# A fused attention and expert kernel: queries, keys and values laid out head dimension first

## The chip, the cores and the metric

The kernel runs on one core of one Trainium2 chip. The metric is the device time of one execution in microseconds (us). The kernel before takes 1295.8 us as the median of 3 runs (1295.32 to 1297.02).

## What is computed

Four batches of 12 heads, 448 tokens, head dimension 64. The scores of all heads are mixed across heads before the softmax (`w_pre`), and the weights again after it (`w_post`). The result feeds a layer of 8 experts, one per token, and then a dense layer of 2048. All arithmetic is in float32.

```python
def _attn_ref(q, k, v, w_pre, w_post):
    scale = 1.0 / np.sqrt(q.shape[-1])
    scores = scale * np.matmul(q, k.transpose(0, 1, 3, 2))
    scores = np.einsum('bhij,hg->bgij', scores, w_pre)
    scores = scores - np.max(scores, axis=-1, keepdims=True)
    attn = np.exp(scores)
    attn = attn / (np.sum(attn, axis=-1, keepdims=True) + 1e-09)
    attn = np.einsum('bhij,hg->bgij', attn, w_post)
    return np.matmul(attn, v).astype(np.float32)

def reference(...):
    attn_out = _attn_ref(**attn_kwargs)
    x = attn_out.transpose(0, 2, 1, 3).reshape(B * S, H * D)
    x = _moe_ref(x=x, **moe_kwargs)      # argmax expert, gate * (relu(x @ w1[e]) @ w2[e])
    return _moe2_ref(x=x, **moe2_kwargs) # (h - tanh(h)) @ w_out, h = x @ w_in
```

## The kernel before, in words

The kernel has four stretches: a prologue (loads, keys of batch 0, the first scores), an attention loop, the experts, and the dense layer. The change touches the prologue and the attention loop alone.

Attention is cut into 16 query tiles T (four per batch, of 120, 120, 120 and 88 queries). For each tile, S (`emit_S`, line 316) makes the scores of two heads at a time as a product of head dimension 64: both heads of pair p lie one above the other on the 128 partitions. To keep float32 accuracy each operand is cut into a rounded part `hi` and a rest `lo`, and three products are added (line 330). The parts come from `tr_k` (line 283, once per batch and pair: 24 calls) and `tr_q` (line 297, two halves per tile: 32 calls). Queries and keys arrive token first, so both turn them on TensorE with an identity (lines 287 and 303; 4 turns in a call of `tr_k`, 3 in one of `tr_q`) into a PSUM bank; ScalarE then copies the bank to `hi` (lines 293, 310) and VectorE subtracts to get `lo` (lines 294, 311).

The scores of 10 queries by 12 heads form a block of 120 rows, which a DMA on SP's queue (`emit_relay`, line 358, kept NSR = 8 blocks ahead) brings into shape. There are NBK = 180 blocks, and the loop (line 1149) runs one step per block. In step s TensorE's program order is: P(s) (line 373: heads mixed with `w_pre`), then one filling (S, or AV: the weighted sum of values, line 430), then T(s-2) (line 412: heads mixed with `w_post` and the block turned, LAG = 2 steps behind), then the turns of that step (`turns`, line 1176), then X (line 464) where one is due. VectorE in a step: the maximum of P(s) (line 377), `emit_W` for block s-1 (lines 387 to 390), a piece of the dense weights' rounding (`conv_do`, lines 117 to 119) in some steps, and the `lo` parts, deferred through `late2`. ScalarE: exp(s) (line 380), the `hi` parts, the copies of T (line 417) and AV (line 432).

Which step does what is written out by hand before the loop: `at(pos, fn, ...)` puts a call into a step, `at_e` into the next step that has no other user of the bank "e". `posS2(T, p)` and `posAV(T, p)` give the steps of S and AV. Lines 1007 to 1015 place the loads of q (6 steps ahead of the tile's first S), the turns of q, the loads of k (5 steps ahead of its turns) and the turns of k. `conv_do` is spread over 72 steps (lines 1035 to 1048), preferring those with AV or S.

The prologue (lines 1114 to 1148) does a little idle work on TensorE (`warm`, line 216, a product of the identity with itself), turns k and q of tile 0, and makes the scores of tile 0 and a third of tile 1. When the last pair of tile 0 is there, `relay_to` starts the first relays.

In the prologue and in the loop alike, q comes in a DMA whose pieces are 64 floats (line 147), and k in two DMAs per pair, one per head (line 152).

## Time and profile before

| | |
|---|---|
| median of 3 runs | 1295.8 us |
| profiled execution, its own time | 1295.99 us |
| its span in the profile | 1294.1 us |
| TensorE busy | 1283.5 us (99%) |
| VectorE busy | 1003.8 us (78%) |
| ScalarE busy | 747.7 us (58%) |
| GpSimd busy | 489.4 us (38%) |
| attention loop | about 19.5 to 500 us of the span |

PE is TensorE's products, PEld its weight loads, which run beside the products; DVE is VectorE, ACT ScalarE, POOL GpSimd, SP the engine that issues most DMAs. The end of a product is modelled in the profile, and products overlap: what a group of products holds up of the next is read from start to start, not from the durations.

### The profile page before, as it was taken

Reading aid. Unit: us, or ns where it says so; the run is one execution under the profiler, and the core shown is the slowest. Engines: PE = TensorE matmul, PEld = TensorE weight load, DVE = VectorE, ACT = ScalarE, POOL = GpSimd, SP = SyncE. Lnnn points to the kernel's source line nnn. Section 1 sums busy time; section 2 is a strip of 40 time slices with the busy share of each in tenths; the row PEclk is TensorE's granted clock in tenths of the full one; section 3 lists DMA queues with packets and bytes.
Section 4 is the critical chain, followed back from the end, with each engine's and each line's share of the span. In section 5 each row is a group of like instructions: output and inputs, shape, how many; then the busy total and the mean of one; then the engine's idle time right before and its main releaser. Section 6 shows DMA issues by size and latency. Waiting matters only on the chain.

```text
span 1294.1 us, 24851 instructions
## 1 busy us (share of the span) xinstructions
PE 1283.5 (99%) x9072; PEld 1125.4 (87%) x9072; DVE 1003.8 (78%) x2168; ACT 747.7 (58%) x1513; POOL 489.4 (38%) x497
## 2 busy tenths in 40 slices
PE   9999999999999999999999999999999999999998
PEld 6777777777777778999999999999999999999997
DVE  5877877787878677788787676788888887888886
ACT  6767666666766665555544545765444556444432
POOL 1334423351344126333223222454644544444431
PEclk9999999999999999999999999999999999999999
DMA  7887665666557458778988876321211123111102
GB/s 172 268 267 214 199 204 152 200 202 192 160 168 223 147 157 301 262 264 250 268 245 259 265 241 210 105 86 49 86 58 65 49 99 122 50 50 49 50 25 88
DMA packets 153077, 210.95 MB, mean 163 GB/s; under 512 B 57686, under 2 KB 113158, under 8 KB 152950
## 3 DMA queue, kind: packets, MB, share of 16 engines
q1 hardware_dynamic: 149680, 195.37, 49.1%
q0 software_dynamic: 2480, 12.19, 2.7%
q8 instruction: 74, 1.21, 0.4%
q10 hardware_dynamic: 790, 1.74, 0.4%
q14 instruction: 53, 0.43, 0.1%
HBM read 135.71 MB, written 35.01 MB: 132 GB/s over the span
## 4 chain that ended last, share of the span: by engine, by line
PE 94%; DVE 2%; DMA 2%; ACT 1%; issue 0%; POOL 0%; SPq 0%; DVEq 0%; POOLq 0%
PE T L412 12%; PE P L373 10%; PE AV L430 6%; PE o L1454 6%; PE o L1452 6%; PE o L1453 6%; PE h L1418 6%; PE h L1417 6%; PE h L1416 6%; PE S L330 5%; PE ypi L706 3%; PE ypi L707 3%; PE ypi L705 3%; PE hi L729 3%; PE hi L730 3%; PE hi L731 3%
## 5 line engine op out<-in xcount | busy, mean ns | idle before, releaser
L412 PEld LDWEIGHTS T<-w,p 120*112 120x112 f32 (+1 forms) x1440 | 166.1, 177 | 59.5 <-issue 46.0
L122 POOL TENSOR_TENSOR cm<-cm,ct 128x256 f32<-128x256 f32 x96 | 70.7, 736 | 313.5 <-DVE ct L119 291.6
L412 PE MATMUL T<-w,p 120*112 120x120 f32 (+1 forms) x1440 | 185.0, 272 | 0.2 <-ACT p L380 0.2
L1399 POOL TENSOR_TENSOR gl<-th,gh 128x512 fp32r<-128x512 f32 (+1 forms) x64 | 77.5, 1211 | 241.1 <-ACT gh L1398 180.4
L373 PE MATMUL P<-sr,wpre 120*120 120x448 f32 x360 | 166.3, 544 | 1.0 <-DMA sr<-ssb 1.0
L380 ACT ACTIVATE p<-P,mx 120x448 f32<-120x448 f32 x180 | 114.1, 634 | 89.9 <-DVE mx L387 76.2
L1420 ACT ACTIVATE u<-h 128x512 f32<-128x512 f32 (+1 forms) x64 | 35.0, 547 | 204.1 <-PE h L1418 204.1
L1452 PE MATMUL o<-woh,gh 128*128 128x384 f32 x448 | 151.4, 338 | 0.0
L1454 PE MATMUL o<-woh,gl 128*128 128x384 f32 x448 | 150.4, 336 | 0.0
L1453 PE MATMUL o<-wol,gh 128*128 128x384 f32 x448 | 150.1, 335 | 0.0
L1458 DVE TENSOR_TENSOR acc<-acc,o 128x384 f32<-128x384 f32 x196 | 106.5, 548 | 47.2 <-PE o L1454 47.2
L377 DVE TENSOR_REDUCE mx<-P 120x1 f32<-120x448 f32 x180 | 111.6, 620 | 28.9 <-PE P L373 26.7
L120 POOL TENSOR_TENSOR cm<-craw 128x256 f32<-128x256 f32 x96 | 66.9, 697 | 112.8 <-DMA craw<-in_moe_w_in 59.2
L417 ACT COPY A<-T 112x480 f32<-112x480 f32 x180 | 102.3, 568 | 9.7 <-PE T L412 9.7
L729 PE MATMUL hi<-xhi,w1h 128*128 128x256 f32 x336 | 95.3, 283 | 0.0
L730 PE MATMUL hi<-xli,w1h 128*128 128x256 f32 x336 | 95.2, 283 | 0.0
L731 PE MATMUL hi<-xhi,w1l 128*128 128x256 f32 x336 | 95.2, 283 | 0.0
L705 PE MATMUL ypi<-w2hi,hhi 128*128 128x384 f32 x272 | 93.9, 345 | 0.0
L430 PEld LDWEIGHTS AV<-A,v 112*64 112x64 f32 x1536 | 73.9, 137 | 21.8 <-issue 10.7
L706 PE MATMUL ypi<-w2li,hhi 128*128 128x384 f32 x272 | 91.2, 335 | 0.2 <-DVE w2li L673 0.2
L707 PE MATMUL ypi<-w2hi,hli 128*128 128x384 f32 x272 | 91.2, 335 | 0.0
L121 POOL TENSOR_SCALAR cm<-cm 128x256 f32<-128x256 f32 x96 | 85.9, 895 | 8.4
(299 smaller groups left out, 3436.3 us busy)
## 6 DMA issues: line engine op xcount, KB each, us to landing
sr<-ssb SPq DMA_DIRECT2D x176, 210.0 KB
r<-in_moe_w SPq DMA_DIRECT2D x72, 384.0 KB
r<-in_moe_w SPq DMA_DIRECT2D x52, 512.0 KB
craw<-in_moe_w_in SPq DMA_DIRECT2D x48, 256.0 KB
craw<-in_moe_w_out SPq DMA_DIRECT2D x48, 256.0 KB
wor<-wo_d SPq DMA_DIRECT2D x16, 768.0 KB
raw<-wi_d SPq DMA_DIRECT2D x15, 768.0 KB
wi_d<-cm SPq DMA_DIRECT2D x48, 128.0 KB
```

The costliest lines, as they stand in the source:

```text
L373: pe.matmul(pt[:n, :S], wpre[:n, :n], t[:n, :], start=True, stop=True)
L412: pe.matmul(pt[:CP, c * n:(c + 1) * n] if m == 10 else pv[:, c], p[:n, c * CP:(c + 1) * CP], w[:n, :] if m == 10 else wv, start=True, stop ...
L430: pe.matmul(pt[64 * hh:64 * hh + 64, x * 120:x * 120 + n], vt[b, p + x][:, hh, c, :], A[T][:, c, 2 * (p + x) + hh, :n], start=c == 0, stop ...
L705: pe.matmul(pt[:, :384], a, wh[:, n0:n0 + 384], start=f == 0, stop=False)
L706: pe.matmul(pt[:, :384], a, wl[:, n0:n0 + 384], start=False, stop=False)
L707: pe.matmul(pt[:, :384], l, wh[:, n0:n0 + 384], start=False, stop=f == KF - 1)
L729: pe.matmul(pt[:, :256], wh[:, sl], xh[:, c, :], start=c == 0, stop=False)
L730: pe.matmul(pt[:, :256], wh[:, sl], xl[:, c, :], start=False, stop=False)
L731: pe.matmul(pt[:, :256], wl[:, sl], xh[:, c, :], start=False, stop=c == KD - 1)
L1452: pe.matmul(pt[:, :384], gh[:, sl], wo[0][:, f, n0:n0 + 384], start=f == 0, stop=False)
L1453: pe.matmul(pt[:, :384], gh[:, sl], wo[1][:, f, n0:n0 + 384], start=False, stop=False)
L1454: pe.matmul(pt[:, :384], gl[:, sl], wo[0][:, f, n0:n0 + 384], start=False, stop=f == GF - 1)
```

## The change

The host lays q, k and v out in the order in which they lie in SBUF: q and k head dimension first, with the two heads of a pair one above the other. Each load is one DMA with long pieces. `tr_q` and `tr_k` keep their names but turn nothing: `hi` is a ScalarE copy of the loaded tile (in the prologue a VectorE copy for q of tile 0), `lo` a VectorE subtraction from it. They no longer use PSUM or TensorE. From tile 3 on they are placed in steps that hold an AV (`at_av`, at most two to a step where there is a choice); there the `hi` copies follow exp(s) directly and the `lo` subtractions follow `conv_do`. q has two buffers instead of one and is loaded 9 steps ahead of its parts, k 8 steps ahead. In the prologue there are more idle products, the scores of each pair are brought to SBUF half by ScalarE and half by VectorE (`both`), and the loads of `w_pre` and `w_post` are issued earlier.

```diff
         def load_k(b, p):
-            t = ap.tile([CP, NJ, 2, D], F32, tag="natk", name=f"natk{b}_{p}", bufs=NP)
-            for hh in range(2):
-                sp.dma_start(t[:, :, hh, :], k[b, 2 * p + hh].rearrange("(p c) d -> p c d", c=NJ))
+            t = ap.tile([128, S], F32, tag="natk", name=f"natk{b}_{p}", bufs=NP)
+            sp.dma_start(t, k[b, p])
...
-        def tr_k(b, p, tag="e"):
-            src = nat.pop(("k", b, p))
-            pt = ps(tag, f"ptk{b}_{p}")
-            for c in range(NJ):
-                pe.transpose(pt[:, c * CP:(c + 1) * CP], src[:, c].rearrange("p h d -> p (h d)"), ident[:CP, :CP])
+        def tr_k(b, p, cpy=act.copy):
+            raw = nat.pop(("k", b, p))
             hi = ap.tile([128, S], F32R, tag="kh", name=f"kh{b}_{p}", bufs=6)
             lo = ap.tile([128, S], F32R, tag="kl", name=f"kl{b}_{p}", bufs=6)
             kT[b, p] = (hi, lo)
-
-            def evac():
-                act.copy(hi, pt[:, :S])
-                return lambda: dve.tensor_sub(lo, pt[:, :S], hi.bitcast(F32))
-            return evac
-
-        def tr_q(T, hf, tag="e"):
+            cpy(hi, raw)
+            return lambda: dve.tensor_sub(lo, raw, hi.bitcast(F32))
+
+        def tr_q(T, hf, cpy=act.copy):
             n = IT[T % 4][1]
-            src = nat["q", T]
-            pt = ps(tag, f"ptq{T}_{hf}")
-            for p in range(3):
-                pp = 3 * hf + p
-                pe.transpose(pt[:, p * 120:p * 120 + n], src[:n, 2 * pp:2 * pp + 2, :].rearrange("p h d -> p (h d)"), ident[:n, :n])
-            pv = pt[:, :360].rearrange("p (c i) -> p c i", c=3)[:, :, :n]
+            raw = nat["q", T][:, 3 * n * hf:3 * n * hf + 3 * n].rearrange("p (c i) -> p c i", c=3)
...
+        avs = {int(posAV(T, p)): 0 for T in range(4 * B - 1) for p in range(0, NP, 2)}
+
+        def at_av(lo, hi, fn, *a):
+            ok = [x for x in sorted(avs) if int(lo) < x < int(hi)]
+            x = ([x for x in ok if avs[x] < 2] + [min(ok, key=lambda x: avs[x])])[0]
+            avs[x] += 1
+            at(x, fn, *a)
+            return x
+
+        for T in range(3, 4 * B):
+            b, it = divmod(T, 4)
+            if it == 0:
+                for p in range(0, 4):
+                    at(at_av(posS2(T - 1, p), posS2(T, p), tr_k, b, p) - 8, load_k, b, p)
+            x = at_av(posS2(T - 1, 2), posS2(T, 0), tr_q, T, 0)
+            at_av(posS2(T - 1, 4), posS2(T, 2), tr_q, T, 1)
+            at(x - 9, load_q, T)
...
-        warm("b", 8)
+        warm("b", 16)
         pen = prep_en()
         next(pen)
-        fns = [tr_k(0, 0, "e"), tr_q(0, 0, "d")]
...
+        tr_q(0, 0, dve.tensor_copy)()
+        tr_k(0, 0)()
+        tr_k(0, 1)()
         for p in range(NP):
+            if p + 2 < NP:
+                tr_k(0, p + 2)()
             if p == 1:
...
-            if p + 2 < NP:
-                tr_k(0, p + 2, "de"[p % 2])()()
-            run_fill(emit_S, (0, p, (None, "cc", "bb")[p % 3]))
+                tr_q(0, 1, dve.tensor_copy)()
+            run_fill(emit_S, (0, p, (None, "cc", "bb")[p % 3], True))
+            warm("e", 3)
             for _ in range(2):
                 if p >= 1:
                     next(pen, None)
+            if p == 3:
+                tr_q(1, 0)()
...
             ex()
+            subs = [fn(*a) for fn, a in todo if fn in (tr_q, tr_k)]
             for fn, a in todo:
                 if fn is conv_do:
                     fn(*a)
+            for fn in subs:
+                fn()
...
-            turns = [x for x in fill if x[0] in (tr_q, tr_k)] if on else []
-            for fn, a in turns:
-                flush("e")
-                late2.append(("e", fn(*a)()))
...
+    def lay(name, a):
+        if name == "q":
+            t = a.reshape(b, h // 2, 2, s, d).transpose(0, 2, 4, 1, 3).reshape(b, 2 * d, h // 2, s)
+            return np.concatenate([t[:, :, :, x].reshape(b, 2 * d, -1) for x in parts], axis=2)
+        if name == "k":
+            return a.reshape(b, h // 2, 2, s, d).transpose(0, 1, 2, 4, 3).reshape(b, h // 2, 2 * d, s)
...
```

## Rows read from the trace of the kernel before

**Rows 1.** The page, part 1: busy time, share of the span, instructions.

```profile
PE 1283.5 (99%) x9072; PEld 1125.4 (87%) x9072; DVE 1003.8 (78%) x2168; ACT 747.7 (58%) x1513; POOL 489.4 (38%) x497
```

**Rows 2.** The page, part 4: the chain that ended last, by engine.

```profile
PE 94%; DVE 2%; DMA 2%; ACT 1%; issue 0%; POOL 0%; SPq 0%; DVEq 0%; POOLq 0%
```

**Rows 3.** Windows, the loop: PE, PEld, DVE, ACT, POOL busy (count), clock, DMA.

```profile
22.00:490.00 468.00, 468.00 (x4071) 349.53 (x4070) 358.10 (x1106) 320.17 (x761) 159.16 (x219) 1.00 0.66 199
```

**Rows 4.** Timeline, weight loads of two steps: start, length, line, tiles, count.

```profile
132.72 0.35 PEld L303 LDWEIGHTS ptq<-ident,natq 120*128 120x128 f32 x3
133.02 0.29 PEld L373 LDWEIGHTS P<-sr,wpre 120*120 120x120 f32 x2
133.97 1.63 PEld L430 LDWEIGHTS AV<-A,v 112*64 112x64 f32 x32 [0.66 <-PE ptq L303]
135.76 0.89 PEld L412 LDWEIGHTS T<-w,p 120*112 120x112 f32 x8 [0.16 <-issue]
136.57 0.29 PEld L373 LDWEIGHTS P<-sr,wpre 120*120 120x120 f32 x2
```

**Rows 5.** Timeline, weight loads: turns of 88 queries, and of a key pair.

```profile
197.27 0.32 PEld L303 LDWEIGHTS ptq<-ident,natq 88*128 88x128 f32 x3
197.53 0.29 PEld L373 LDWEIGHTS P<-sr,wpre 120*120 120x120 f32 x2
...
199.10 0.44 PEld L287 LDWEIGHTS ptk<-ident,natk 112*128 112x128 f32 x4
199.49 0.29 PEld L373 LDWEIGHTS P<-sr,wpre 120*120 120x120 f32 x2
```

**Rows 6.** Groups by line, 22 to 490 us: count, busy us, mean ns, idle.

```profile
L303 PE MATMUL ptq<-ident,natq 120*128 120x120 f32 (+1 forms) x84 | 12.6, 259 | 0.0
L287 PE MATMUL ptk<-ident,natk 112*128 112x112 f32 x72 | 9.9, 259 | 0.0
```

**Rows 7.** Timeline, VectorE: maximum, weights of a block, a rounding piece.

```profile
132.16 0.62 DVE L377 TENSOR_REDUCE mx<-P 96x1 f32<-96x448 f32 x1 [0.37 <-PE P L373]
...
133.07 0.28 DVE L390 TENSOR_SCALAR w<-wpost,mx 120x120 f32<-120x120 f32 x1
...
135.53 0.28 DVE L117 TENSOR_SCALAR ct<-craw 128x256 int32<-128x256 int32 x1
...
136.30 0.42 DVE L119 SCALAR_TENSOR_TENSOR ct<-craw,ct 128x256 int32<-128x256 int32 x1
```

**Rows 8.** Lines 293, 294, 310, 311: ns min/median/max, first and last start.

```profile
L293 ACT CAST kh<-ptk x24: 522/526/533, 6.4 to 351.6; 128x448 fp32r<-128x448 f32 x24
L294 DVE TENSOR_TENSOR kl<-ptk,kh x24: 602/625/627, 7.0 to 352.1; 128x448 fp32r<-128x448 f32 x24
L310 ACT CAST qh<-ptq x32: 379/450/465, 6.9 to 444.8; 128x360 fp32r<-128x360 f32 x24, 128x264 fp32r<-128x264 f32 x8
L311 DVE TENSOR_TENSOR ql<-ptq,qh x32: 431/532/533, 7.5 to 445.3; 128x360 fp32r<-128x360 f32 x24, 128x264 fp32r<-128x264 f32 x8
```

**Rows 9.** Lines 669, 673, the same work from SBUF, in the experts.

```profile
L669 DVE CAST w1h<-r x4: 681/686/1225, 487.3 to 496.2; 128x1024 fp32r<-128x1024 f32 x4
...
L673 DVE TENSOR_TENSOR w1l<-r,w1h x50: 1209/1219/1661, 501.3 to 788.6; 128x1024 fp32r<-128x1024 f32 x50
```

**Rows 10.** Timeline, the prologue: idle products, first turns, Exp, scores, relays, P(0).

```profile
1.43 3.49 PEld L220 LDWEIGHTS warm<-ident 128*128 128x128 f32 x16 [1.43 <-POOL dmask L174]
...
5.63 0.55 PEld L287 LDWEIGHTS ptk<-ident,natk 112*128 112x128 f32 x4 [0.72 <-DMA natk<-in_k]
5.69 0.20 ACT L261 ACTIVATE mxk<-carry 128x1 f32<-128x1 f32 x1
...
15.94 0.62 DVE L335 TENSOR_SCALAR ssb<-S 120x448 f32<-120x448 f32 x1
...
16.63 6.54 SPq L360 DMA_DIRECT2D sr<-ssb  x8
...
19.54 1.74 PE L373 MATMUL P<-sr,wpre 120*120 120x448 f32 x4 [1.02 <-DMA sr<-ssb]
```

More of the change, by code (lines that the diff above doesn't have):

```diff
@@ L30, in body @@
 @with_exitstack
-def body(ctx: ExitStack, tc, q, k, v, w_pre, w_post, emb, tau, w1, w2, win, wout, out):
+def body(ctx: ExitStack, tc, q, k, v, w_pre, w_post, emb, tau, w1, w2, win, wout, out, dims):
     nc = tc.nc
     pe, act, dve, pool, sp = nc.tensor, nc.scalar, nc.vector, nc.gpsimd, nc.sync
-    B, H, S, D = q.shape
+    B, H, S, D = dims
     NT = B * S
@@ L163, in body @@
         load_k(0, 0)
+        load_k(0, 1)
         load_q(0, 1)
-        for p in range(1, NP):
+        for p in range(2, NP):
             load_k(0, p)
+        load_q(1)
+        wr = cp.tile([120, 2, H], F32, name="wr")
+        sp.dma_start(wr[:, 0, :], w_pre.rearrange("(o h) g -> o h g", o=1).to_broadcast([10, H, H]))
+        sp.dma_start(wr[:, 1, :], w_post.rearrange("(o h) g -> o h g", o=1).to_broadcast([10, H, H]))
         act.dma_start(xbuf[1][:E], emb)
@@ L169, in body @@
         make_identity(nc, ident)
-        wr = cp.tile([120, 2, H], F32, name="wr")
         dmask = a2.tile([120, 120], F32, tag="w", name="dmask", bufs=3)[:, :10]
@@ L307, in tr_q, with emit_S @@
             qT[T, hf] = (hi, lo)
-            def evac():
-                act.copy(hi[:, :, :n], pv)
-                return lambda: dve.tensor_sub(lo[:, :, :n], pv, hi[:, :, :n].bitcast(F32))
-            return evac
+            cpy(hi[:, :, :n], raw)
+            return lambda: dve.tensor_sub(lo[:, :, :n], raw, hi[:, :, :n].bitcast(F32))
         s_sb = {}
-        def emit_S(T, p, two=None):
+        def emit_S(T, p, two=None, both=False):
             b, it = divmod(T, 4)
@@ L332, in evac @@
             def evac():
-                if two:
+                if two or both:
                     act.activation(s_sb[T][:n, 2 * p, :], pts[0][:n, :S], AF.Copy, scale=SCALE)
@@ L1007, in body @@
         for T in range(2, 4 * B):
-            at(posS2(T, 0) - 6, load_q, T)
-            at_e(posS2(T, 0) - 2, tr_q, T, 0)
-            at_e(posS2(T, 2) - 2, tr_q, T, 1)
-        for b in range(1, B):
-            for p in range(NP):
-                e = posS2(4 * b - 1, p) + 1
-                at(e - 5, load_k, b, p)
-                at_e(e, tr_k, b, p)
+            if T == 2:
+                at(1, load_q, T)
+                at(int(posS2(T, 0)) - 2, tr_q, T, 0)
+                at(int(posS2(T, 2)) - 2, tr_q, T, 1)
+        avs = {int(posAV(T, p)): 0 for T in range(4 * B - 1) for p in range(0, NP, 2)}
[13 more added lines that the diff above has]
+            at(x - 9, load_q, T)
+            if it == 0:
+                for p in range(4, NP):
+                    at(at_av(posS2(T - 1, p), posS2(T, p), tr_k, b, p) - 8, load_k, b, p)
         for p in range(NP):
@@ L1040, in body @@
         mid = [k for k in free if emit_S2 in kinds(k) and emit_AV2 not in kinds(k)]
-        alone = [k for k in long_ if not {emit_X, tr_q, tr_k} & set(kinds(k))]
+        alone = [k for k in long_ if emit_X not in kinds(k) and (tr_q not in kinds(k) and tr_k not in kinds(k))]
         more = CA - len(long_) - len(mid)
@@ L1139, in body @@
         at_e(4, tr_en)
-        PEF = (tr_q, tr_k, emit_S, emit_S2, emit_AV2, emit_X, tr_en)
-        for fn in [f() for f in (tr_q(1, 0, "e"), tr_q(1, 1, "d"))]:
-            fn()
+        PEF = (emit_S, emit_S2, emit_AV2, emit_X, tr_en)
+        tr_q(1, 1)()
         for p in range(2):
@@ L1182, in body @@
             for x in fill:
-                if x not in turns:
-                    run_fill(*x)
+                run_fill(*x)
             for fn, a in todo:
@@ L1614 @@
     from concourse.bass_utils import run_bass_kernel_spmd
+    b, h, s, d = inputs["q"].shape
+    parts = [slice(i, min(i + 120, s)) for i in range(0, s, 120)]
+    def lay(name, a):
[4 more added lines that the diff above has]
+            return a.reshape(b, h // 2, 2, s, d).transpose(0, 1, 2, 4, 3).reshape(b, h // 2, 2 * d, s)
+        if name == "v":
+            return a.reshape(b, h // 2, 2, s // 112, 112, d).transpose(0, 1, 4, 2, 3, 5).reshape(b, h // 2, 112, -1)
+        return a
     nc = bacc.Bacc("TRN2", target_bir_lowering=False, num_devices=1)
```

23 lines of the change are left out of this document (6 added, 17 removed).

## Prediction, written before the result was known

> **What bounds the kernel now.** First the busy times: TensorE is busy 99% of the span, no other engine over 78% [rows 1]. Busy products can be late products, so the chain that ended last comes second: 94% of it is TensorE, and DVE, DMA and ACT together hold 5% [rows 2]. Third the loop alone, 22 to 490 us, since the change lies there: in 468 us TensorE never stood still, VectorE worked 358.1 us (77%) and ScalarE 320.2 us (68%), at a granted clock of 1.00, the upper level of 2.4 GHz [rows 3]. What remains is whether the products stand back to back or wait for each other's operands. The timeline shows the first: in a step the weight loads of turns, P, AV, T and the next P follow at 132.72, 133.02, 133.97, 135.76 and 136.57 [rows 4]. The operands of T are there long before: the block's weights in rows 7 are ready at 133.07 + 0.28 = 133.35, and the T that reads them loads at 135.76, a margin of 2.4 us [rows 4, 7]. So in the loop TensorE's program order is the time, and an instruction taken out of it is worth the time from its start to the next one's start.
>
> **What the turns cost.** Three readings of the same rows differ, and the choice among them is the prediction. The mean duration is 259 ns for both kinds, 72 + 84 turns in the loop [rows 6], which would be 156 x 0.259 = 40.4 us. The busy time, with overlaps counted once, is 12.6 + 9.9 = 22.5 us [rows 6]. From start to start, the three turns of a 120-query half put off the next P by 133.02 - 132.72 = 0.30 us [rows 4], three of an 88-query half by 197.53 - 197.27 = 0.26 us, four of a key pair by 199.49 - 199.10 = 0.39 us [rows 5]. I take the last, because the next product doesn't wait for the end of a turn: P's weights load beside the last turns. In the loop are 84 / 3 = 28 halves of q (tiles 2 to 15: 20 of 120 queries and 8 of 88) and 72 / 4 = 18 key pairs. The sum: 20 x 0.30 + 8 x 0.26 + 18 x 0.39 = 6.0 + 2.1 + 7.0 = 15.1 us. The rest of the turns lie in the prologue, below.
>
> The Trainium skill, page "TensorE: Matmul & The Clock Gate", section "Part 4: PE-mode transpose", gives about 275 ns for a 128x128 transpose inside a kernel. Our mean of 259 ns agrees with that as a duration [rows 6]; taken as the price of one, an estimate by the page is 156 x 0.275 = 42.9 us of gain. The rows above speak against that: four turns took 0.39 us of the order [rows 5].
>
> **What takes their place in the loop.** The `hi` copies and `lo` subtractions were there before, from PSUM; now they read SBUF and stand elsewhere. From PSUM a key's `hi` takes 0.526 us, its `lo` 0.625, a query half's 0.450 and 0.532 (the 88-query halves 0.38 and 0.43, the lower ends) [rows 8]. For `lo` from SBUF the nearest row is the 1024-column subtraction with 1.219 us [rows 9], or 1.19 ns a column; the key's from PSUM is 0.625 / 448 = 1.40. By the first a key's `lo` is at least 0.53 us, by the second 0.625; I take 0.625, since the 360-column row, 1.48 ns a column, shows a fixed part that weighs more in short ones. So the work of both engines stays as it is, within 0.1 us an instruction either way.
>
> It matters where it stands. An AV step on TensorE lasts 136.57 - 133.02 = 3.55 us [rows 4]. The heaviest common load of VectorE in one is a maximum and the making of a block's weights (from 132.16 to 133.35: 1.19), a rounding piece (135.53 to 136.72: 1.19) and two key subtractions (1.25): 3.63 us [rows 7, 8]. This is level with the step, and the steps beside it hold no `lo` any more; a backlog of 1.25 us at most meets a margin of 2.4 us. ScalarE gets two copies of 0.53 us behind exp(s), ahead of the copies of AV and T, in a step of 3.55 us; at 68% it has the room. I cost both at nothing. They are hidden by the AV products. If that cover were gone, all subtractions in the loop would be on the path: 18 x 0.625 + 20 x 0.532 + 8 x 0.43 = 25.3 us.
>
> A new wait is that of ScalarE for the load itself: the `hi` copy waits for k or q, and behind it on ScalarE are the copies of AV and T, then the next exp, for which T and P wait. The loads are issued 8 or 9 steps ahead, some 21 us (the 468 us of rows 3 hold about 176 steps, 2.66 us each); the first keys had landed by 5.63 us, issued within that time [rows 10]. Nothing. On SP a pair's k is one issue instead of two and nothing is moved past the relays but loads that find their buffer free (q has two), so P's relays start no later. Placing X earlier, where it no longer shares the bank "e" with turns, moves work without adding any.
>
> **Prologue.** Before, the first turn waits for keys (5.63), the last scores reach SBUF at 15.94 + 0.62 = 16.56, the relays are issued at 16.63 and P(0) starts at 19.54 [rows 10]. Now no turn stands ahead of the scores, but ScalarE can't make the first `hi` before the table load and the Exp of line 261 are through, at 5.69 + 0.20 = 5.89 [rows 10]. From the first key's `hi` (5.89 + 0.53 = 6.42) VectorE has six key subtractions (6 x 0.62), six halves of scores (6 x 0.62, where it had four), for the second half of q a copy (0.34: half of 0.686 for 1024 columns, since 360 is about a third and something is fixed [rows 9]) and a subtraction (0.53), one subtraction of tile 1 (0.53), and some 1.3 us of small operations for the norms of the experts: 3.7 + 3.7 + 0.9 + 0.5 + 1.3 = 10.1, so 16.5 us if it never waits. Before it was 16.56. The turns go, and VectorE is late next: a gain of zero. Bounds: 0.7 us of gain if it gets by with shorter copies and the norms fall into gaps; a loss of 1.5 us if scores arrive late behind the added idle products. I take zero; the value nearest to the rows is that of a VectorE without gaps.
>
> **The sum.** The rows are of an execution of 1295.99 us (span 1294.1), 0.2 us over the median of 1295.8. 1295.99 - 15.1 + 0 + 0 = 1280.9, by the median 1280.7; I say 1281. What follows the loop (experts, dense) hangs on the loop's last steps and moves forward with them. Bounds of the unknown: prologue -0.7 to +1.5; three places where a tile's q is prepared one step before its first S (tiles 4, 8, 12), with 0.53 us each if VectorE is behind, 0 to 1.6; the first expert weights, loaded in the last steps, which may land relatively later, 0 to 1; runs scatter by 1.7 us. Own range of the forecast: 1279 to 1284.
>
> **The rivals.**
> 1. A turn costs its duration: the gain is 40.4 us, 1255.6. For it: the durations [rows 6]. Against it: the starts [rows 4, 5], and it would need 54 us of TensorE's time in 192 turns of the whole kernel where the starts show no room for that.
> 2. VectorE becomes the bound in AV steps (slower). Its place is the AV step with two parts and a rounding piece; the price is all `lo` subtractions on the path, 25.3 - 15.1 = 10.2 us more than before: 1306.2. It decides from the point where VectorE's load in such a step is over 3.55 + 2.4 us. For it: the load is 3.63 us already, and SBUF operations of VectorE run at times far over their median, the 1024-column subtraction up to 1.661 us, the copy up to 1.225 instead of 0.686 [rows 9]. Against it: two subtractions at 1.36 times their time add 0.45 us, not 2.3, and 77% leaves VectorE idle time in the neighbours.
> 3. It is exposed in part, in the six to nine steps that hold two key parts and in the steps where S, AV and two parts meet: 0.5 to 1 us each in some fifteen steps, 8 to 15 us back, 1288 to 1296: smaller gain or none.
> 4. The prologue gets worse and the clock falls: TensorE has less to do there, and an idle stretch ahead of P(0) (1.02 us waiting now [rows 10]) may grow to 2 or 3. At the kernel's start sixteen idle products took 3.49 us, 0.22 each [rows 10], where four turns of like size later took 0.39 together [rows 5]: the clock's lower level (1.2 GHz). A stretch of that length at half speed again would cost 3.49 / 2 = 1.7 us: 1282.7. This lies in the forecast's range.
> 5. The change doesn't take TensorE's time away, because the order is held by something else, such as exp (P needs a bank that exp two steps before has read): 1295.8. Against it the margins above.
>
> **How the numbers follow.** Forecast (with rival 4) 0.87; rival 3 0.05; rival 2 0.03; rival 5 0.02; rival 1 or another larger gain 0.03. The forecast alone holds more than 0.8, so the range is its own, widened to 1278 below for a prologue that gains and a loop in which neighbours of the turns also close up, and to 1285 above: 1278 to 1285. Two runs of this kernel can be told apart from 0.2%, 2.6 us: faster 0.94, same 0.03, slower 0.03.
>
> **What would show it.** Right: no rows of lines 287 and 303 on TensorE; loop gaps between P, AV and T as before, at 0.95, 1.79 and 0.81 us; the loop from P(0) to the last T some 15 us shorter; P(0) at 19 to 21 us; VectorE's share of the loop near 79%. Wrong: TensorE's weight loads waiting for `w` or P for exp in AV steps (rival 2, 3), P(0) after 21.5 us, or a loop shorter by 20 us and more (rival 1).

## The result, and the profile after

The changed kernel takes 1286.9 us as the median of 4 runs (1283.95 to 1287.94), the kernel before 1296.4 in 4 runs beside it (1295.32 to 1299.89): a ratio of 0.9918, with a 95% interval of 0.9893 to 0.9944. That is faster, by some 9.5 us where 15.1 were forecast, and 1.9 us above the forecast's range. The execution profiled took 1287.94 us, with a span of 1286.2.

The page of the kernel after, part 1 (busy time, share of the span, instructions) and part 4 (the chain that ended last, by engine), and its windows of the loop (PE, PEld, DVE, ACT, POOL busy with counts, granted clock, DMA share, GB/s), which answer to [rows 1 to 3]:

```profile
PE 1270.6 (99%) x8914; PEld 1110.2 (86%) x8914; DVE 1013.5 (79%) x2172; ACT 746.5 (58%) x1511; POOL 497.0 (39%) x497
...
PE 86%; DVE 5%; DMA 5%; ACT 2%; issue 1%; POOL 1%; SPq 0%; POOLq 0%; DVEq 0%; ACTq 0%
...
22.00:490.00 468.00, 465.10 (x4049) 342.38 (x4048) 373.30 (x1131) 327.21 (x778) 177.63 (x231) 1.00 0.64 206
```

TensorE's part of the chain fell from 94% to 86%, that of VectorE and of DMA rose from 2% to 5% each. In the loop TensorE now stands still for 2.9 us, where it never did, and VectorE works 373.3 us instead of 358.1. So the turns are gone, and something else now ends last in places.

Weight loads of one AV step in the kernel after, which answer to [rows 4]:

```profile
113.70 0.29 PEld L362 LDWEIGHTS P<-sr,wpre 120*120 120x120 f32 x2
114.64 1.63 PEld L419 LDWEIGHTS AV<-A,v 112*64 112x64 f32 x32 [0.66 <-ACT p L369]
116.43 0.89 PEld L401 LDWEIGHTS T<-w,p 120*112 120x112 f32 x8 [0.16 <-DVE w L379]
117.25 0.29 PEld L362 LDWEIGHTS P<-sr,wpre 120*120 120x120 f32 x2
```

The step is as it was without its turns: 0.94 us from P to AV, 1.79 to T, 0.82 to the next P. Here nothing is late.

Who waited for whom in the loop, 22 to 482 us, TensorE's products (us in total, times, longest):

```profile
PE T L401 <- DVE w L379: 1.3, 5, 0.3
PE S L319 <- DVE lg L458: 1.2, 3, 0.6
```

The kernel before has no line in this view. The distance from the start of one group of products to the start of the next, against the median for the same two groups in the same trace, says more than the idle time (all that is over 0.12 us late, from P(0) to the last T). T behind P is 0.50 us late at 118.92, 238.92 and 358.91 us (starts of P), 0.31 at 338.96, 0.32 and 0.30 behind the P of a block of 96 rows at 127.77 and 367.77, and 0.19 and 0.38 in the last two steps. T behind S is 0.78, 0.78 and 1.06 late near 166, 286 and 407 us, where S had to wait for the bank of X. Together 5.6 us. The kernel before has 1.7 us: 0.34 to 0.38 three times behind S, and 0.13, 0.14 and 0.38 behind P.

Where these places lie tells two kinds apart. T behind P at 118.92, 238.92, 338.96 and 358.91 us comes two or three steps after a step with a rounding piece and two query parts: 1.8 us. The three T behind S and the two behind blocks of 96 rows come two steps after a step with two rounding pieces and no part: 3.2 us. The change itself put those pieces there: a second piece goes only into steps without parts, and the parts have moved (second pieces before in steps 15, 35, 45, 80, 90, 125, 135 and 162, now in 42, 45, 56, 90, 101, 132, 146 and 162).

The durations of the parts (ns min/median/max, first and last start), which answer to [rows 8]:

```profile
L291 ACT CAST kh<-natk x24: 548/564/583, 5.8 to 345.0; 128x448 fp32r<-128x448 f32 x24
L292 DVE TENSOR_TENSOR kl<-natk,kh x24: 603/626/1154, 6.4 to 345.7; 128x448 fp32r<-128x448 f32 x24
L300 ACT CAST qh<-natq x30: 397/481/494, 13.9 to 422.3; 128x360 fp32r<-128x360 f32 x22, 128x264 fp32r<-128x264 f32 x8
L301 DVE TENSOR_TENSOR ql<-natq,qh x32: 424/527/1060, 4.5 to 422.8; 128x360 fp32r<-128x360 f32 x24, 128x264 fp32r<-128x264 f32 x8
```

The medians of the subtractions are those of before; the longest are not: 13 of the 56 take over 0.7 us, up to 1.154, where the longest was 0.627. Each of the 13 is 0.53 us longer than the others of its kind, and each lies across the end of one GpSimd operation (line 122) and the start of the next (line 120). The 24 that lie beside line 122 alone are not longer.

One late T with what stands ahead of it. First TensorE, then VectorE, then GpSimd (start, length):

```profile
117.35 0.92 PE L362 MATMUL P<-sr,wpre 120*120 120x448 f32 x2
...
118.92 0.92 PE L362 MATMUL P<-sr,wpre 120*120 120x448 f32 x2
120.17 1.04 PE L401 MATMUL T<-w,p 120*112 120x120 f32 x8 [0.33 <-DVE w L379]
...
115.67 0.63 DVE L379 TENSOR_SCALAR w<-wpost,mx 120x120 f32<-120x120 f32 x1
116.22 0.28 DVE L117 TENSOR_SCALAR ct<-craw 128x256 int32<-128x256 int32 x1
...
117.41 1.50 DVE L301 TENSOR_TENSOR ql<-natq,qh 128x360 fp32r<-128x360 f32 x2
118.84 0.61 DVE L366 TENSOR_REDUCE mx<-P 120x1 f32<-120x448 f32 x1
...
119.74 0.28 DVE L379 TENSOR_SCALAR w<-wpost,mx 120x120 f32<-120x120 f32 x1
...
115.61 0.61 POOL L120 TENSOR_TENSOR cm<-craw 128x256 f32<-128x256 f32 x1
116.31 0.90 POOL L121 TENSOR_SCALAR cm<-cm 128x256 f32<-128x256 f32 x1
117.64 0.88 POOL L122 TENSOR_TENSOR cm<-cm,ct 128x256 f32<-128x256 f32 x1 [0.44 <-DVE ct L119]
```

Two query subtractions take 1.50 us instead of some 1.0, the `w` ahead of them 0.63 instead of 0.28, both while GpSimd works. The P at 117.35 gets its maximum only at 118.84; behind this maximum in VectorE's order, at 119.74, comes the `w` of the block before, and the T of that block waits for it.

The prologue (TensorE's scores and idle products, VectorE's last half of scores, SP's relays, P(0)), which answers to [rows 10]:

```profile
7.58 0.47 PE L319 MATMUL S<-kh,qh 64*120 64x448 f32 x2
...
8.38 0.94 PE L223 MATMUL warm<-ident 128*128 128x128 f32 x6
9.25 0.47 PE L319 MATMUL S<-kh,qh 64*120 64x448 f32 x2
...
16.85 0.62 DVE L324 TENSOR_SCALAR ssb<-S 120x448 f32<-120x448 f32 x1 [0.86 <-PE S L319]
...
17.56 4.09 SPq L349 DMA_DIRECT2D sr<-ssb  x5
...
20.42 1.83 PE L362 MATMUL P<-sr,wpre 120*120 120x448 f32 x4 [1.37 <-DMA sr<-ssb]
```

A pair's scores follow each other every 1.67 us, with 0.87 us of idle products between them, and VectorE waits for S. P(0) starts 0.88 us later than before.

In stretches, from the profiled executions: to P(0) 20.42 us (19.54 before), from P(0) to the last T 466.83 us (478.56), from there to the end 798.95 (795.98). So +0.9, -11.7 and +3.0.

### The profile page after: what moved, and what is told of

It is laid out like the page before. It is cut to its first block, busy times and chain, and to the rows that moved or that the text cites. A ratio compares the mean times of both kernels' runs of the same rounds, so it can differ in the third digit from the quotient of the medians.

```text
span 1286.2 us, 24544 instructions
## 1 busy us (share of the span) xinstructions
PE 1270.6 (99%) x8914; PEld 1110.2 (86%) x8914; DVE 1013.5 (79%) x2172; ACT 746.5 (58%) x1511; POOL 497.0 (39%) x497
## 4 chain that ended last, share of the span: by engine, by line
PE 86%; DVE 5%; DMA 5%; ACT 2%; issue 1%; POOL 1%; SPq 0%; POOLq 0%; DVEq 0%; ACTq 0%
PE T L401 10%; PE P L362 8%; PE o L1452 6%; PE o L1450 6%; PE o L1451 6%; PE h L1415 6%; PE h L1416 6%; PE h L1414 6%; PE AV L419 5%; PE S L319 5%; PE ypi L695 3%; PE ypi L696 3%; PE ypi L694 3%; PE hi L718 3%; PE hi L720 3%; PE hi L719 3%
## 5 line engine op out<-in xcount | busy, mean ns | idle before, releaser
L122 POOL TENSOR_TENSOR cm<-cm,ct 128x256 f32<-128x256 f32 x96 | 76.9, 801 | 299.9 <-DVE ct L119 267.3
L120 POOL TENSOR_TENSOR cm<-craw 128x256 f32<-128x256 f32 x96 | 69.8, 727 | 109.0 <-DMA craw<-in_moe_w_in 56.5
```

## The experiments

The loop below is always the time from the start of P(0) to the start of the last T, in one profiled execution.

**The parts in the old steps.** All of the change, but parts, loads, X and rounding where the kernel before has them, and `lo` deferred as there.

```diff
-        for T in range(3, 4 * B):
...
-            x = at_av(posS2(T - 1, 2), posS2(T, 0), tr_q, T, 0)
+        for T in range(2, 4 * B):
+            at(posS2(T, 0) - 6, load_q, T)
+            at_e(posS2(T, 0) - 2, tr_q, T, 0)
...
-            for fn in subs:
-                fn()
+                    late2.append(("e", fn(*a)))
```

> The changed kernel, but with the parts of q and k (and their loads, X and the rounding pieces) in the steps of the kernel before, and the lo subtractions deferred as there; no turns. From the start of P(0) to the last T the kernel before takes 477.9 us and the changed one 466.2. Theory A (a turn is worth its time from start to start, 15.1 us in the loop; what is missing was lost by the new places): 462.9 +- 0.7 here. Theory B (the turns are worth only some 11.7 us, since the engines beside TensorE are level with it once they are gone, wherever the parts stand): 466 again. The prologue is the changed kernel's, P(0) at 20.4 us; device time by A about 3 us under the changed kernel's, 1284, by B equal to it, 1287.

1285.4 us in 6 runs, ratio 0.9915 (0.9900 to 0.9931), the same as the change. The loop took 466.44 us, as long as with the new steps (theory B's number), not 462.9. No subtraction is longer than 0.626 us, and T still waits for `w` (six times, 1.2 us of idle time). The subtractions here, from SBUF as in the change:

```profile
L292 DVE TENSOR_TENSOR kl<-natk,kh x24: 603/624/626, 6.4 to 342.9; 128x448 fp32r<-128x448 f32 x24
...
L301 DVE TENSOR_TENSOR ql<-natq,qh x32: 426/532/536, 4.5 to 433.7; 128x360 fp32r<-128x360 f32 x24, 128x264 fp32r<-128x264 f32 x8
```

27 of those in the loop lie beside GpSimd's work, none across line 122 and line 120. So a loss of this size needs neither the new places of the parts nor long subtractions, though the late T stand in other steps here.

**No two rounding pieces ahead of X.**

```diff
-        alone = [k for k in long_ if emit_X not in kinds(k) and (tr_q not in kinds(k) and tr_k not in kinds(k))]
+        alone = [k for k in long_ if emit_X not in kinds(k) + kinds(k + 1) and (tr_q not in kinds(k) and tr_k not in kinds(k))]
```

> The changed kernel with one difference: the rounding pieces that stand twice in a step are no longer put into a step ahead of an X (steps 56, 101 and 146 hold one piece instead of two; 42, 45, 87, 90, 132, 135, 162 and 166 hold two). Theory A1 (the waits of S for the bank of X, 0.48, 0.48 and 0.76 us, and the three late T behind them come from VectorE's second piece): these are gone, from P(0) to the last T 466.2 - 2.3 = 463.9. Rival (they come from the parts of q prepared nearby): the waits stay, 466.2.

1286.2 us, ratio 0.9920 (0.9905 to 0.9934). The waits of S behind X at 165, 285 and 405 us went: they came from the two pieces in the steps ahead of X. But a new one came, P to T at 454.99 us, 1.39 us later than usual, behind a step that now has two pieces, and one of 0.32 behind another such step; the loop took 466.15. The waits behind steps with two query parts stayed (0.49 us).

**No idle products between the scores.**

```diff
             run_fill(emit_S, (0, p, (None, "cc", "bb")[p % 3], True))
-            warm("e", 3)
```

> The changed kernel without the three idle products behind each pair's scores in the prologue. Theory A2 (they hold up the scores, and so VectorE): P(0) at 19.2 to 19.6 us instead of 20.42, device time 0.9 lower. Rival 1 (VectorE is the bound of the prologue): P(0) stays at 20.3 to 20.5. Rival 2 (without them the clock falls): P(0) as by A2, but the first steps of the loop slow, at the lower clock, up to 2 us lost again. From P(0) on 466.2 in A2 and rival 1.

P(0) started at 18.18 us, 2.24 us earlier. But the clock fell. P(0) in this kernel, and the window from 17.6 to 21 us (the column behind POOL is the granted clock):

```profile
18.18 3.31 PE L362 MATMUL P<-sr,wpre 120*120 120x448 f32 x4 [2.61 <-DMA sr<-ssb]
...
17.60:21.00 3.40, 2.81 (x4) 1.12 (x4) 0.62 (x1) 0.30 (x1) 0.00 (x0) 0.56 0.68 257
```

TensorE's last scores end at 15.6 us, and it had nothing to do until 18.18; from 18.0 us its granted clock was at the lower level (1.2 GHz). The first four products of P took 3.31 us instead of 1.83, and the loop 468.66. Two times lay at 1285.5 and 1285.7 (mean granted clock 0.996 and 0.997, one of them the execution shown), four at 1288.8 to 1290.7 (0.995); the median is 1289.2, ratio 0.9940 (0.9923 to 0.9957): nothing is gained. The idle products cost 2.2 us of P(0), and without them the clock fell.

**GpSimd's three rounding operations of the loop left out**, in the changed kernel and, as a control, in the kernel before (weights under 3.4e-5 are not set to zero). Besides, VectorE's result `ct` gets four buffers instead of two and is itself what the DMA stores.

```diff
-        pool.tensor_mul(m, raw[:, :, 1].bitcast(F32), raw[:, :, 1].bitcast(F32))
-        pool.tensor_single_scalar(m, m, 3.4332275390625e-05 ** 2, op=ALU.is_ge)
-        pool.tensor_mul(m, m, t.bitcast(F32))
+        if j >= CONV_A:
+            pool.tensor_mul(m, raw[:, :, 1].bitcast(F32), raw[:, :, 1].bitcast(F32))
+            pool.tensor_single_scalar(m, m, 3.4332275390625e-05 ** 2, op=ALU.is_ge)
+            pool.tensor_mul(m, m, t.bitcast(F32))
+        else:
+            m = t.bitcast(F32)
```

> The changed kernel with GpSimd's three operations of a rounding piece left out in the attention loop (weights of under 3.4e-5 are not set to zero). Theory A3 (the lo subtractions are stretched, up to 1.15 us, because they now read both operands from SBUF while GpSimd works): no lo subtraction in the loop over 0.64 us, the late T at steps 41, 86 and 131 gone; together with the shorter rounding steps of VectorE from P(0) to the last T 463 +- 0.7. Rival (they are stretched by something else, such as the loads): still up to 1.1 us, 466.

> Edit: the kernel before, with GpSimd's three rounding operations of the attention loop left out (weights under 3.4e-5 are not set to zero), as the control for the changed kernel without them (loop 461.83 us). Theory A (the difference of the two loops is then the price of the turns alone, 15.1 us; GpSimd costs the kernel before nothing, since its subtractions read PSUM and are never above 0.63 us): loop 477.0 to 478.5 (478.56 with GpSimd), difference to the changed kernel without GpSimd 15.2 to 16.7 us. Rival B (GpSimd slows VectorE in the kernel before as well, by its maxima and rounding pieces): loop 475 or less, so that the turns are worth 13 us or less and the rest of what was gained without GpSimd is not theirs.

VectorE and GpSimd from 22 to 478 us: windows of the kernel before, of the same without GpSimd, of the change, of the change without GpSimd (columns as above):

```profile
22.00:478.00 456.00, 456.00 (x3951) 340.47 (x3950) 349.11 (x1071) 312.58 (x742) 157.33 (x216) 1.00 0.65 197
...
22.00:478.00 456.00, 455.85 (x3950) 340.22 (x3949) 327.92 (x1071) 314.44 (x744) 0.00 (x0) 1.00 0.65 198
...
22.00:478.00 456.00, 453.34 (x3903) 332.64 (x3904) 365.18 (x1107) 319.65 (x761) 166.63 (x217) 1.00 0.63 202
...
22.00:478.00 456.00, 455.78 (x3944) 335.68 (x3941) 343.09 (x1121) 323.19 (x771) 6.05 (x8) 1.00 0.65 208
```

GpSimd's work costs VectorE 349.11 - 327.92 = 21.2 us of longer instructions in the kernel before. For the change the windows don't hold the same work (1107 instructions with GpSimd, 1121 without), so the durations of the whole loop are added up by kind: `w` 65.8 us with GpSimd and 51.2 without, the rounding's SCALAR_TENSOR_TENSOR 67.9 and 61.2, the subtractions 32.2 and 25.1, together 28.4 us. (The kernel before: 65.9 and 51.2, 67.9 and 61.2, 25.3 and 25.3, together 21.4.) The profile of the change lists no wait of VectorE for GpSimd in the loop, so what GpSimd costs lies in the instructions.

Before, that was free: the loop without GpSimd took 478.46 us, with it 478.56. After, it was not: 461.83 without, 466.83 with it. The T that was late at 119 us:

```profile
118.34 0.92 PE L365 MATMUL P<-sr,wpre 120*120 120x448 f32 x2
119.09 1.02 PE L404 MATMUL T<-w,p 120*112 120x120 f32 x8
```

It comes 0.75 us behind P, as usual. Of the 5.6 us of late starts 0.65 are left, so their difference is the 5.0 us of the loop.

So without GpSimd the turns are worth 478.46 - 461.83 = 16.6 us, and 466.83 - 461.83 = 5.0 us were given back once GpSimd slows VectorE. The times: 1282.4 us, ratio 0.9891 (0.9873 to 0.9910), for the change; 1298.5 in one run for the kernel before, whose part behind the loop took 2 us more that time.

Which instructions GpSimd slows is told by their lines. The block's weights `w` (from SBUF), in the kernel before and in the same without GpSimd, and the key subtraction of the change without GpSimd:

```profile
L390 DVE TENSOR_SCALAR w<-wpost,mx x180: 278/283/783, 22.4 to 495.4; 120x120 f32<-120x120 f32 x176, 96x120 f32<-96x120 f32 x4
...
L393 DVE TENSOR_SCALAR w<-wpost,mx x180: 278/282/527, 23.0 to 495.9; 120x120 f32<-120x120 f32 x176, 96x120 f32<-96x120 f32 x4
...
L295 DVE TENSOR_TENSOR kl<-natk,kh x24: 601/620/627, 6.4 to 341.9; 128x448 fp32r<-128x448 f32 x24
```

In the kernel before 41 of the 180 `w` take over 0.35 us, without GpSimd in the loop nearly none. The maximum, which reads PSUM, is never above 0.63 us, and so were the subtractions as long as one operand was in PSUM [rows 8].

**Parts first.** The `hi` copies ahead of exp(s), the subtractions ahead of the rounding piece.

```diff
-            ex()
             subs = [fn(*a) for fn, a in todo if fn in (tr_q, tr_k)]
+            ex()
+            for fn in subs:
+                fn()
             for fn, a in todo:
                 if fn is conv_do:
                     fn(*a)
-            for fn in subs:
-                fn()
```

> Edit: in a step of the loop the hi copies stand ahead of exp(s) on ScalarE, and the lo subtractions ahead of the rounding piece on VectorE, so that GpSimd's three operations of that piece begin only after the subtractions. Theory A (the subtractions that read both operands from SBUF are stretched while GpSimd works, up to 1.154 us instead of 0.627, and this makes w late for T): the long subtractions become fewer (sum of all lo in the kernel 38.1 us falls to 33 or less), the waits of T for w near 119, 239 and 359 us (+0.50 each) and 339 us (+0.31) go, the loop from P(0) to the last T falls from 466.8 to about 465; the waits of S behind X near 165, 285 and 405 us (0.5 to 0.76 each) stay, since they come from two rounding pieces ahead of X. Time about 1285. Rival B (VectorE has simply too much to do in a step with AV, two parts and a rounding piece, 3.63 us against 3.55, whatever the order): the subtractions may get shorter, but T waits for w at the same places, loop 466.5 to 467. Rival C: the hi copies ahead of exp(s) delay exp, P and T wait for it: loop 467 to 469.

A miss for theory A. The subtractions were short again (sum 31.5 us, as in the kernel before 31.1; the longest 0.721), yet T waited at the same places (0.51 us near 119, 239 and 359 us, 0.31 near 219 and 339), the loop took 467.33 us and the median was 1287.2, ratio 0.9925 (0.9903 to 0.9948). VectorE around the first of them:

```profile
115.83 0.63 DVE L379 TENSOR_SCALAR w<-wpost,mx 120x120 f32<-120x120 f32 x1
116.38 1.17 DVE L301 TENSOR_TENSOR ql<-natq,qh 128x360 fp32r<-128x360 f32 x2
...
119.50 0.70 DVE L379 TENSOR_SCALAR w<-wpost,mx 120x120 f32<-120x120 f32 x1
```

GpSimd's operations now lie beside another `w`, which takes 0.70 us instead of 0.28: at this place what was saved on the subtractions is lost on the next instruction that reads SBUF. Over the kernel the subtractions fell by 6.6 us and all `w` rose by 2.4 (65.8 to 68.2), so VectorE had less work, and the loop was no shorter (466.83 and 467.94 us in two executions of the change). The loop is in rival C's range too, but T waits for `w` here, not for exp. Long subtractions are not what the late T come from; which steps VectorE is behind in is.

**Idle products behind the last scores** instead of between them.

```diff
-            warm("e", 3)
...
         for _ in pen:
             pass
+        warm("e", 8)
```

> Edit: the three idle products behind each pair's scores in the prologue are left out, and eight idle products are put behind the last scores of the prologue, ahead of P(0). Theory A (the idle products between the scores hold up the scores and so the relays; what they give is the clock, and for that they can stand in the gap ahead of P(0) as well): P(0) starts at 18.2 us instead of 20.4 as without idle products, the granted clock stays at 1.00 from 15 to 24 us, the loop is as long as that of the changed kernel (466.8, where without idle products it was 468.7): 2.2 us less than the changed kernel, about 1284.7. Rival B (eight products of 0.29 us leave a gap, or the clock falls for want of earlier work): the granted clock is at the lower level for some stretch between 17 and 24 us and the loop is 1 to 2 us longer: 1286 to 1287. Rival C: the idle products end after the first relays have landed, P(0) at 18.5 to 19.

P(0) at 18.66 us, right behind the last idle product and 0.48 later than with none (rival C's number), the loop 466.67: 1.8 us of what idle products cost between the scores are gained, and the loop loses nothing. The clock did fall once, but earlier than theory A's window, in the last scores, whose products then followed each other every 0.37 us instead of 0.20:

```profile
7.00:12.00 5.00, 3.92 (x30) 2.57 (x29) 4.25 (x11) 3.95 (x9) 0.00 (x0) 1.00 0.45 160
...
13.00:16.20 3.20, 2.94 (x17) 2.43 (x16) 3.17 (x9) 1.76 (x4) 0.83 (x1) 0.50 0.00 0
16.20:19.60 3.40, 3.31 (x23) 2.27 (x20) 1.08 (x2) 0.94 (x2) 1.12 (x3) 0.99 0.45 174
```

1285.2 us, ratio 0.9912 (0.9890 to 0.9934): 1.7 us under the change in the median, 1.8 in P(0). The two intervals overlap, so the gain rests on the trace.

**All three**: parts first, idle products last, and the eight doubled rounding pieces in steps that are long or have none behind them.

```diff
-        steps = sorted(long_ + mid + [alone[i * len(alone) // more] for i in range(more)])
+        steps = sorted(long_ + mid + [42, 45, 60, 87, 90, 105, 132, 135])
```

> Edit: the changed kernel with the parts ahead of exp and the rounding piece, with the idle products behind the last scores of the prologue, and with the eight doubled rounding pieces in steps 42, 45, 60, 87, 90, 105, 132 and 135 (long steps, or steps followed by one without rounding) instead of 42, 45, 56, 90, 101, 132, 146 and 162. Theory A (three separate losses of the changed kernel: late scores in the prologue 2.2 us, stretched subtractions some 2 us, S behind X 1.7 us): P(0) at 18.2, the loop 462 to 463 from P(0) to the last T, no wait of TensorE above 0.4 us in it; with 795 to 799 us after the loop some 1279 to 1280. Rival B (VectorE's load, not its order): the loop stays at 465 to 467, 1282 to 1285.

1282.7 us in 6 runs, ratio 0.9895 (0.9876 to 0.9914). P(0) at 18.51; the waits of S behind X are gone, the five of T for `w` (0.51 three times, 0.31, 0.22) are not, nor three of 0.32 behind blocks of 96 rows, and the loop is 464.84: between the theories' numbers, nearer to B's.

**No piece in the six steps with AV and two query parts**, on top of the last.

```diff
-        steps = sorted(long_ + mid + [42, 45, 60, 87, 90, 105, 132, 135])
+        two = [k for k in long_ if kinds(k).count(tr_q) == 2]
+        steps = sorted([k for k in long_ if k not in two] + mid + [42, 45, 60, 87, 90, 105, 132, 135, 52, 97, 142, 150, 162, 166])
```

> Edit: the kernel with all three edits before (parts first, idle products last in the prologue, other doubled steps), and now no rounding piece in the six steps with AV and two query parts (31, 39, 76, 84, 121, 129); their pieces are second ones in steps 52, 97, 142, 150, 162 and 166. Theory A (what is left in the loop are places where VectorE, slowed by GpSimd, has a piece in one step, a piece and two parts in the next, and plain steps behind: T waits for w at 117.22, 236.53 and 356.16 us with 0.51 each, 336.21 with 0.31, 41.94 with 0.22): these five waits go, the loop from P(0) to the last T falls from 464.84 to 462.8 to 463.3, median some 1281. Rival B (VectorE's load over some ten steps is what counts, so a piece moved makes another step late): new waits of T for w behind steps 52, 97, 142, 150, 162 or 166, the loop at 464 to 466.

Rival B. The three waits of 0.51 went, those of 0.31 and 0.22 stayed (0.31 and 0.28), and new ones came behind the steps that took the pieces: 0.43 us each at 153.87, 273.14 and 392.64, and 1.36 at 452.99. The loop took 466.05 us. TensorE there:

```profile
452.99 0.92 PE L362 MATMUL P<-sr,wpre 120*120 120x448 f32 x2
455.10 1.05 PE L401 MATMUL T<-w,p 120*112 120x120 f32 x8 [1.19 <-DVE w L379]
```

The median, 1282.1 us in 5 runs, ratio 0.9879 (0.9861 to 0.9896), is level with that of the version before it. Both lie 4 to 5 us under the changed kernel, with intervals that still touch its own; the traces show 1.9 and 1.4 us of that in P(0) and 2.0 and 0.8 in the loop, the rest lies behind the loop, where the scatter is as large.

**Both kernels once more**, for the scatter behind the loop, with no edit.

> Edit: none, the kernel before once more, for the scatter of what follows the loop. Theory A (the waits behind the loop are for gathers and loads whose landing scatters in both kernels): the loop within 0.3 us of 478.56, the time from the last T to the end anywhere between 795 and 799 us (795.98 in the execution shown, 798.04 without GpSimd in the loop), its differences in the waits of TensorE at the first gathered rows near 518 us, at the expert weights, and at the gathered results near 803 us. Rival B (the change costs something there): 795.5 to 796.5 again.

> Edit: none, the changed kernel once more, for the same scatter. Theory A: the loop within 0.3 us of 466.83 with the same waits of T and S at 119, 165, 239, 285, 339, 359 and 405 us, and behind it 795 to 799 us. Rival B (the change costs something behind the loop): 798 to 799 again.

One run each: 1296.9 and 1286.3 us. The kernel before: loop 478.57, behind it 797.11 us (795.98 in the execution shown). The change: loop 467.94, behind it 796.40 (798.95). So the 3 us behind the loop are not the change's: the same part took 2.6 us less the second time. The loop itself varied by 1.1 us, more than expected, by waits of the same kind. What TensorE waited for from 500 to 1285 us, in the second execution of the kernel before, then in the first and the second of the change:

```profile
PE xty L691 <- DMA yg<-y_d,sgn: 2.0, 1, 2.0
...
PE xty L680 <- DMA yg<-y_d,sgn: 2.2, 1, 2.2
...
PE xti L678 <- DMA xgi<-x_d,ids: 1.1, 1, 1.1
PE xty L680 <- DMA yg<-y_d,sgn: 0.2, 1, 0.2
```

The wait for the gathered results `yg` comes and goes in both. A wait for the first gathered rows `xgi` stands in both executions of the change (0.3 and 1.1 us) and in neither of the kernel before. It isn't the change's either: the kernel before without GpSimd's work in the loop has it (0.4), and of the versions of the changed kernel three don't (the parts in the old steps, all three edits, and the next one).

**The cover put back.** One idle product on TensorE behind T for each part made in the step.

```diff
                 T_mm(i, 0, NJ)
                 flush("d")
+            for fn, a in todo:
+                if fn in (tr_q, tr_k):
+                    flush("e")
+                    warm("e", 1)
```

> Edit: the changed kernel, and behind T in each step of the loop one idle product on TensorE for each query half or key pair whose parts are made there (46 products of some 0.27 us from start to start, 12.4 us together, where the turns took 0.26 to 0.39 each). Theory A (what the turns took of TensorE was time in which VectorE, slowed by GpSimd, caught up): with two products back in the steps ahead of the late T, the waits of T for w near 119, 239 and 359 us (0.49 each) and 219 and 339 us (0.31 each) shrink to 0.1 or nothing, and the loop grows by less than the products take, from 466.8 to 467.9 us to 477 to 478. The waits of S behind X (0.48, 0.48, 0.76) stay, since no parts are made in those steps. Rival B (those waits don't hang on TensorE's time, since VectorE's chain of maxima and weights moves with it): they stay at 0.3 to 0.5, and the loop is 479.2 to 480.3.

The place that was late at 119 us, now 3 us later (P at 117.35 is P at 122.47 here):

```profile
121.69 0.94 PE L223 MATMUL warm<-ident 128*128 128x128 f32 x4
122.47 0.92 PE L362 MATMUL P<-sr,wpre 120*120 120x448 f32 x2
...
124.04 0.92 PE L362 MATMUL P<-sr,wpre 120*120 120x448 f32 x2
124.89 1.05 PE L401 MATMUL T<-w,p 120*112 120x120 f32 x8
```

Without the added products the second P to T was 1.25 us; with them it is 0.85, 0.10 above the usual 0.75. The three waits of 0.50 fell below 0.13, as theory A said; two of 0.31 near 219 and 339 us, which it had said would go, were there, as were the waits of S behind X and of the T behind blocks of 96 rows, and a wait of 1.64 us came at 495.66, in the last steps. The sum was mis-sized: two idle products in a row hold up P by 0.78 us, not 0.54, so all 46 cost 16.3 us from start to start, and the loop took 483.53 (+16.7 or +15.6 against the two executions of the change), the whole 1305.0. That time of TensorE's is cover for VectorE is shown at three places; over the whole loop it gave nothing net.

## Why the prediction was wrong

**What bounds the kernel: right, for the kernel before.** TensorE's program order was the time there: without GpSimd VectorE worked 21 us less, and the loop stayed the same within 0.1 us.

**What the turns cost: right.** The choice of the starts over the durations holds: 16.6 us without GpSimd in the loop, where the sum said 15.1 and the durations 40.4. The starts of all 46 groups of turns in the loop of the kernel before add up to 15.0 us. Of the 1.5 us beyond 15.1, 1.3 are late starts that the kernel before has without GpSimd and the change without GpSimd hasn't (1.9 and 0.65 us by the measure above). One figure beside it was wrong: 192 turns at 0.259 us are 49.7 us, not the 54 of rival 1; nothing hangs on it.

**What takes their place: this step failed.** The prediction said of the parts in AV steps "I cost both at nothing. They are hidden by the AV products." Measured in place of nothing: 5.0 us (6.1 by the second execution of the change). Three things in it were wrong.

First, the load of an AV step, 3.63 us, was added up from undisturbed instructions, a `w` of 0.28 us among them. With GpSimd at work `w` takes up to 0.78 and a rounding instruction up to 0.92, in the kernel before already: 21.2 us of VectorE's time that no step of the sum held.

Second, the margin of 2.4 us was read at the T of the AV step. The T that came late are those of the plain steps behind it, where P to T is 0.75 us and the backlog of two or three steps arrives together, and those behind the second rounding pieces, which the change had moved and the prediction didn't look at. Before, the time of the turns was cover for VectorE's backlog: GpSimd's toll on VectorE cost the loop 0.1 us with the turns and 5.0 without them.

Third, it put that "the work of both engines stays as it is, within 0.1 us an instruction either way". For ScalarE that held (0.564 us a key's `hi` instead of 0.526, 0.481 a query half's instead of 0.450). For VectorE the median held and 13 instructions did not, up to 1.154 us. The row with such times was read, the expert's subtraction from SBUF at 1.209 to 1.661 [rows 9], but only its low end was used for the term, and its high end was put aside in rival 2 as 0.45 us. This third error is real but did not make the loss: with the parts in the old steps no subtraction was long, and the loop was as long.

The Trainium skill, page "SBUF — State Buffer", section "Who interferes with whom", says why one might have looked closer at the subtractions: a VectorE instruction with two SBUF inputs contends with a GpSimd instruction that reads SBUF, one with a single SBUF input outside the two-port modes doesn't. The change turns 46 subtractions in the loop from the second kind into the first. The runs agree as far as they go: 0.627 us at most with one operand in PSUM, 1.154 with both in SBUF, 0.627 again without GpSimd; but of the 38 that lay beside GpSimd's work only 13 were longer by more than 0.2 us.

**Rival 3 came nearest, with the wrong place and size**, at a chance of 0.05: VectorE is exposed in part. It put 0.5 to 1 us in some fifteen steps with parts, 8 to 15 us back; measured were 0.2 to 1.1 us in some ten places, most of it behind second rounding pieces, which it didn't name, 5.0 us back.

**Prologue: the number nearly right, the reason wrong.** Zero was predicted for P(0), within -0.7 to +1.5, and it was +0.88 in both pairs of executions (20.42 to 19.54, 20.22 to 19.34). But VectorE was not "late next": it waited for S, which stood behind the idle products in TensorE's order. The prediction had this as the reason of its upper bound and not of its value. Without these products P(0) is 2.2 us earlier, and then the falling clock, rival 4's second half, takes most of it back: 1.7 us were estimated for it, and the loop was 1.8 us longer (0.7 against the second execution of the change), the first four products of P alone 1.5. That the two numbers agree owes something to luck: the estimate came from the idle products at the kernel's start, for which the granted clock in the profile's windows is 1.00; the lower level there can only be inferred (the weight loads of eight idle products took 3.49 us there and 1.86 at a granted 0.99 in the kernel with the idle products behind the last scores).

**Behind the loop: "moves forward with it", right within the scatter.** 795.98 and 797.11 us before, 798.95 and 796.40 after.

**The sum as it came out**: -16.6 (turns) + 5.0 (VectorE slowed by GpSimd, no longer covered) + 0.9 (prologue) = -10.7 us up to the last T, by profiled executions. Behind it came +3.0 in the first pair of executions (-8.0 in all) and -0.7 in the second (-10.6); by the medians it is -9.5.

## What to carry to other kernels

What a removed instruction is worth is read from start to start in the program order of the engine that bounds, but only until the next engine's chain ends later: add up that engine's load with the longest durations its lines show beside its neighbours, over several steps, and read the margin at the step with the shortest distance. What is taken away may have been the time in which another engine caught up. When an operand moves from PSUM to SBUF, look who else reads SBUF at that time; and look what else the change moves, such as work placed by a rule that avoids the steps it uses. Idle products belong where their engine would wait anyway, not in the order ahead of the work that all wait for.

## What the runs showed of the hardware

A VectorE subtraction of 448 columns with one operand in PSUM never took over 0.627 us beside GpSimd; with both in SBUF it took up to 1.154, but only where it lay across the end of one GpSimd operation on two operands and the start of another (13 times, 0.53 us each). With the subtractions short again (6.6 us less), `w` took over 2.4 us of it.

TensorE's clock fell to its lower level after quite different histories: without idle products in the wait of 2.61 us ahead of P(0); with idle products moved, from about 13 to 16.2 us, when it had waited for no more than 0.97 us at a time since 7 us and had worked 3.92 of the 5 us ahead of 12. Of the two later kernels whose prologue has the same order as each other, the one with all three edits fell too, from about 12.1 to 15.5 us, and the one with no piece in the six steps kept 1.00 from 7 to 24 us.

Two idle products in tiles of their own, one behind the other, held up the next product by 0.78 us, one alone by 0.23; three in one tile in the prologue took 0.87.
